# Three one-pass products of 12-bit parts in place of Strassen's float32 products, in a scan followed by a SiLU feed-forward block

## The chip, the cores and the metric

The kernel runs on one core of one Trainium2 chip. The metric is the device time of one execution in microseconds (us). The core's engines are TensorE (PE, with its weight loads listed as PEld), VectorE (DVE), ScalarE (ACT), GpSimd (POOL) and SyncE (SP), whose queue issues most DMAs. Each engine takes its instructions in program order; semaphores tie them together. SBUF is the on-chip memory of 128 partitions, PSUM holds what TensorE writes.

## The reference

A chunked state-space scan, and a two-layer block with SiLU on its output. Cut to what is computed:

```python
x: (4, 8, 768, 32)   a: (4, 8, 768)   B, C: (4, 8, 768, 16)   # batch, heads, tokens, ...
for c in range(768 // 32):                      # per batch and head
    cum = np.cumsum(log(clip(a[c], 1e-6, 1)))
    M = (C[c] @ B[c].T) * np.exp(cum[:, None] - cum[None, :]) * causal
    y[c] = M @ x[c] + (C[c] @ state) * np.exp(cum)[:, None]
    state = exp(cum[-1]) * state + (B[c] * exp(cum[-1] - cum)[:, None]).T @ x[c]
X = y.transpose(0, 2, 1, 3).reshape(3072, 256)
h = X @ w_in                                    # w_in (256, 2048), given in float64
out = (h * sigmoid(h)) @ w_out                  # w_out (2048, 256), given in float64
```

All but the two weight matrices is float32.

## The kernel before, in words

The 3072 tokens are 12 units of 256 tokens (three per batch); two units that follow each other are a pair, so there are six pairs, 0 to 5. For each unit a scan makes the features x tokens matrix XM; then the first product (256 to 2048 features), SiLU, and the second product (2048 to 256).

**Weights.** They arrive as 16 pieces of float64 (`load_w`), and each is turned into float32 by `w_size` (two ScalarE passes) and `w_bits` (three VectorE instructions, L176 to L180, and an add on GpSimd, L184).

**Scan of a unit.** `f_T` or `f_TP` transposes B and C, `f_P` (L285, L291) and `f_E` (L322, L304) make decays by scans on VectorE, `f_B` (L341) and `f_C` (L373) scale B and C, `f_G` and `f_D0` are the products C·B (L406) and the state's increments (L391), `f_M` (L417) multiplies decays in, `f_S` and `f_SM` carry the state, `f_Y` (L460, L469) gives y and `f_X` (L482) copies it out of PSUM. All products of `f_G` of a unit stand in one tile `gy` of four PSUM banks.

**The two products.** Units 0 to 3 have plain first products, `f_s1` (L505, SiLU in L507). Pairs 2 to 5 take their first product by `f_x1` (L703) in Strassen's way: 7 products for 8, with differences of weights (`f_SW`) and of inputs (`f_XT`, L686, GpSimd), copies out of PSUM (L717), sums on VectorE (L706) and SiLU (L709). Every pair's second product is Strassen's too, `s2_pair` (L648; L611 for the first two of pair 0): 7 x 8 products, sums of weights (`f_SO`, L533) and of activations (`f_T1`, L544, and `f_TS`, L553, which adds by DMAs on GpSimd's queue), copies (L588) and sums of results (`p_add`, L558), then a transpose (L564) and four DMAs per output block on SP's queue (`f_out`). All are float32 products over 256 tokens.

**Order.** The order is written out by hand; no scheduler moves anything. The second product of pair P runs between the first products of pair P+1, and the scans of pair P+2's units are spread over the same stretch by `scan_plan`. From pair 2 on, one round of eight j's per pair does all of it.

`busy` (L226, L228) issues bf16 products at the start whose results are not used.

Of the kernel before, what the change touches and what calls it, by code (L numbers as in the profile page):

```python
# [9 lines left out]
U32 = mybir.dt.uint32  # L10
BF16 = mybir.dt.bfloat16
# [6 lines left out]
MOST = 2.0 ** 16 * (1.875 - 2.0 ** -22)  # L18


@with_exitstack
def kernel(
# [22 lines left out]
    nc = tc.nc  # L45
# [13 lines left out]
    loads = ctx.enter_context(tc.tile_pool(name="loads", bufs=3))  # L59
    loads2 = ctx.enter_context(tc.tile_pool(name="loads2", bufs=2))  # L60
    rawp = ctx.enter_context(tc.tile_pool(name="rawp", bufs=7))
    wtp = ctx.enter_context(tc.tile_pool(name="wtp", bufs=3))
    sc = ctx.enter_context(tc.tile_pool(name="sc", bufs=1))
    sc2 = ctx.enter_context(tc.tile_pool(name="sc2", bufs=2))
    xmp = ctx.enter_context(tc.tile_pool(name="xmp", bufs=4))
    gpool = ctx.enter_context(tc.tile_pool(name="gpool", bufs=4))
    tpool = ctx.enter_context(tc.tile_pool(name="tpool", bufs=1))
    ppool = ctx.enter_context(tc.tile_pool(name="ppool", bufs=5))
    opool = ctx.enter_context(tc.tile_pool(name="opool", bufs=2))
    ps_s = ctx.enter_context(tc.tile_pool(name="ps_s", bufs=1, space=bass.MemoryType.PSUM))  # L70
    ps_h = ctx.enter_context(tc.tile_pool(name="ps_h", bufs=3, space=bass.MemoryType.PSUM))
    ps_o = ctx.enter_context(tc.tile_pool(name="ps_o", bufs=1, space=bass.MemoryType.PSUM))

    ctx.enter_context(tc.manual_schedule())


# [5 lines left out]
    def load_pa(u, q):  # L82

        b, t0 = at(u)
        pa[u] = loads.tile([128, UT], FP32, name="pa")
        q.dma_start(out=pa[u], in_=bass.AP(tensor=a.tensor, offset=a.offset + b * H * S + t0,
                                           ap=[[S, H], [0, N], [1, UT]]))

    def load_ab(u, q):

        b, t0 = at(u)
        ab[u] = loads2.tile([128, 2, H, Q], FP32, name="ab")
# [7 lines left out]

# [9 lines left out]

# [7 lines left out]
    def load_x(u, q):  # L118
        b, t0 = at(u)
        xt[u] = loads.tile([128, 2, H, D], FP32, name="xt")  # L120
# [14 lines left out]
    w_in_sb = const.tile([128, KC, d_ff], FP32, name="w_in_sb")  # L135
    w_out_sb = const.tile([128, NF, d_model], FP32, name="w_out_sb")
# [3 lines left out]
    W = [("i", j) for j in range(8)] + [("o", j) for j in range(8)]  # L140
    RAW = 7
    raw, wu, wv = {}, {}, {}

    def w_piece(n):
        which, j = W[n]
        if which == "i":
            return wi[:, :, j * WF:(j + 1) * WF], w_in_sb[:, :, j * WF:(j + 1) * WF]
        return wo[:, 2 * j:2 * j + 2], w_out_sb[:, 2 * j:2 * j + 2]

    def load_w(n, q):  # L150
        src, dst = w_piece(n)
        if src.dtype == FP32:
            q.dma_start(out=dst, in_=src)
            return
        t = raw[n] = rawp.tile([128, 2, WF, 2], U32, name="raw")
        q.dma_start(out=t.rearrange("p k f two -> p k (f two)"), in_=src.bitcast(U32))

    def w_size(n, what="uv"):  # L160
        if n in raw:
            if "u" in what:
                u = wu[n] = wtp.tile([128, 2, WF], FP32, name="wu")
                nc.scalar.activation(u, raw[n][:, :, :, 1].bitcast(FP32), AF.Abs)
            if "v" in what:
                v = wv[n] = wtp.tile([128, 2, WF], FP32, name="wv")

                nc.scalar.activation(v, raw[n][:, :, :, 0], AF.Copy, scale=2.0 ** -51, bias=2.0)

    def w_bits(n, parts=1):  # L170
        dst = w_piece(n)[1]
        if n in raw:
            u, v, hi = wu.pop(n), wv.pop(n).bitcast(U32), raw[n][:, :, :, 1]


# [3 lines left out]

            nc.vector.scalar_tensor_tensor(out=v, in0=hi, scalar=0x80000000, in1=v,  # L180
                                           op0=ALU.bitwise_and, op1=ALU.bitwise_or)
            for i in range(parts):
                fs = slice(WF // parts * i, WF // parts * (i + 1))
                nc.gpsimd.tensor_tensor(out=dst[:, :, fs].bitcast(U32), in0=u[:, :, fs], in1=v[:, :, fs], op=ALU.add)  # L184
        if n + RAW < len(W):
            load_w(n + RAW, nc.sync)


    A0, A1 = 96, 96 + S // Q
    early = gpool.tile([128, NF, UT], FP32, name="gT")  # L190
    ach = early[:, 0:2].rearrange("p a (h t) -> p (a h) t", t=Q)
    nc.sync.dma_start(out=ach[A0:A1], in_=bass.AP(tensor=a.tensor, offset=a.offset, ap=[[Q, S // Q], [S, H], [1, Q]]))

    flat = early.rearrange("p f t -> p (f t)")
    QZ = 8 * (Q + 1)
    pa01 = flat[:, 6 * UT:8 * UT]
    pz01, one01, pfx01 = (flat[:, 8 * UT + QZ * i:8 * UT + QZ * (i + 1)] for i in range(3))
# [16 lines left out]

# [4 lines left out]

    idle = early[:, 4].bitcast(BF16)  # L220
    nc.vector.memset(idle, 0.0)

    def busy(n, small=0):
        t = ps_o.tile([128, 512], FP32, name="o_ps")
# [7 lines left out]
    sel = early[:, 2:4].rearrange("p a (s c t) -> p (a s) c t", s=2, c=2)  # L232
# [4 lines left out]
    diag1 = early[:, 5:6, 0:Q]  # L237
    nc.vector.memset(diag1, 0.0)
    nc.vector.memset(pz01.rearrange("p (c t) -> p c t", c=8)[:, :, 0:1], 0.0)
    nc.vector.memset(one01, 0.0)  # L240
    nc.vector.memset(one01.rearrange("p (c t) -> p c t", c=8)[:, :, 0:1], 1.0)
# [24 lines left out]
    pz = const.tile([128, 4, Q + 1], FP32, name="pz")  # L266
    one = const.tile([128, 4, Q + 1], FP32, name="one")
    for t, n in ((pz, 0.0), (one, 1.0)):
        nc.gpsimd.memset(t, 0.0)
        if n:  # L270
            nc.gpsimd.memset(t[:, :, 0:1], n)
    E, M, BT, BH, CT, CE, CW, PFX, ST, SM, DP, XM, GTS, BX = ({} for _ in range(14))


    def f_P01():

        nc.vector.tensor_scalar(out=pz01.rearrange("p (c t) -> p c t", c=8)[:, :, 1:],
                                in0=pa01.rearrange("p (c t) -> p c t", c=8), scalar1=1.0, scalar2=1e-6,
                                op0=ALU.min, op1=ALU.max)
# [728 lines left out]
```

## Time and profile before

| what | value |
|---|---|
| median of three runs | 351.29 us (350.81 to 354.5) |
| span of the profiled execution | 348.7 us |
| PE / PEld / DVE / ACT / POOL busy | 98 / 83 / 59 / 47 / 32 % of the span |
| granted TensorE clock, mean | 1.000 |
| HBM read, written | 22.70 MB, 3.15 MB |
| DMAs under 512 B, of all packets | 102424 of 117056 |
| first product of pair 0's second layer (L611) | at 50.5 us |
| last matmul group (L626) starts, ends | 342.8, 345.6 us |

The span runs from the first to the last instruction of one execution; it is the only time that the page gives for that execution, and the median of the runs is 2.6 us above it. Busy time of PE counts pipelined matmuls, so two that follow each other overlap in it; the distance between starts tells their rate. Each float32 matmul of the program stands in the trace as two records.

### The profile page before, as it was taken

What the parts mean: (1) busy time and instruction counts of PE and PEld (TensorE: products, weight loads), DVE (VectorE), ACT (ScalarE), POOL (GpSimd) and SP (SyncE); (2) the same over time, 40 slices, a digit from 0 to 9 for tenths busy, and PEclk for the clock granted to TensorE, in tenths of its full rate; (3) what the DMA queues carried; (4) which work ended last, traced back from release to release, by engine and by line L of the source; (5) the groups of instructions that cost most, each with busy time, mean ns of one, the idle gap of its engine ahead of it and who ended that gap; (6) DMA issues with size and microseconds to landing.
All of it is one profiled execution on the core that took longest, in us unless ns stands there. A gap on an engine that the chain in (4) does not pass through costs nothing.

```text
span 348.7 us, 8382 instructions
## 1 busy us (share of the span) xinstructions
PE 342.7 (98%) x3324; PEld 288.5 (83%) x3324; DVE 204.6 (59%) x406; ACT 162.8 (47%) x399; POOL 113.0 (32%) x140
## 2 busy tenths in 40 slices
PE   8999999999999999999999999999999999999996
PEld 3678888888888888888888888888888888888886
DVE  7998799976795664544663563564652241233912
ACT  3578395323323545455645454644545454454010
POOL 4355245444285032244042244042235112041200
DMA  6877997799857598948178965056604237512202
GB/s 130 203 237 174 241 313 126 132 199 218 144 102 126 124 186 149 169 102 138 21 159 163 187 112 90 16 98 125 115 2 75 39 60 144 107 24 53 41 7 46
DMA packets 117056, 42.66 MB, mean 122 GB/s; under 512 B 102424, under 2 KB 108824, under 8 KB 117016
## 3 DMA queue, kind: packets, MB, share of 16 engines
q1 hardware_dynamic: 110472, 25.73, 35.8%
q0 software_dynamic: 4464, 16.25, 25.0%
q8 instruction: 26, 0.43, 0.6%
q10 hardware_dynamic: 2080, 0.13, 0.4%
q14 instruction: 14, 0.11, 0.1%
HBM read 22.70 MB, written 3.15 MB: 74 GB/s over the span
## 4 chain that ended last, share of the span: by engine, by line
PE 96%; DVE 1%; issue 1%; POOL 1%; ACT 0%; DVEq 0%; POOLq 0%
PE o_ps L648 36%; PE hp L703 28%; PE hp L505 16%; PE hp L648 3%; PE gy L469 2%; PE gy L406 2%; PE o_ps L611 2%; PE gy L460 2%; PE gy L391 1%; PE hp L626 1%; PE hp L312 1%; PE o_ps L226 1%; POOL w_in_sb L184 1%; DVE E L417 0%; PE o_ps L228 0%
## 5 line engine op out<-in xcount | busy, mean ns | idle before, releaser
L706 DVE TENSOR_TENSOR gT<-hp,p 128x256 f32<-128x256 f32 x64 | 26.9, 420 | 73.6 <-ACT p L717 37.6
L648 PE MATMUL o_ps<-gT,w_out_sb 128*128 128x256 f32 x240 | 60.4, 379 | 0.0
L709 ACT ACTIVATE gT<-gT 128x256 f32<-128x256 f32 x96 | 39.7, 414 | 43.9 <-DVE gT L706 43.9
L505 PE MATMUL hp<-XM,w_in_sb 128*128 128x256 f32 x256 | 59.3, 381 | 0.9 <-ACT XM L482 0.5
L505 PEld LDWEIGHTS hp<-XM,w_in_sb 128*128 128x128 f32 x256 | 48.0, 190 | 8.7 <-POOL w_in_sb L184 1.4
L703 PE MATMUL hp<-raw 128*128 128x256 f32 x192 | 52.7, 380 | 0.0
L558 POOL TENSOR_TENSOR ps<-ps 128x256 f32<-128x256 f32 x35 | 29.6, 845 | 71.1 <-ACT ps L588 69.8
L648 PEld LDWEIGHTS o_ps<-gT,w_out_sb 128*128 128x128 f32 x240 | 45.4, 190 | 6.3
L553 POOL DMA_DIRECT2D gT<-gT x31 | 27.9, 929 | 65.7 <-DVE TN L544 21.5
L703 PEld LDWEIGHTS hp<-raw 128*128 128x128 f32 x192 | 36.2, 190 | 5.4 <-POOL ps L558 0.6
L717 ACT ACTIVATE p<-hp 128x256 f32<-128x256 f32 x64 | 24.6, 384 | 27.4 <-PE hp L703 25.9
L706 DVE TENSOR_TENSOR gT<-hp,u 128x256 f32<-128x256 f32 x32 | 13.6, 424 | 38.6 <-PE hp L703 38.6
L703 PE MATMUL hp<-XM,w_in_sb 128*128 128x256 f32 x128 | 34.1, 389 | 0.0
L507 ACT ACTIVATE gT<-hp 128x512 f32<-128x512 f32 x32 | 18.9, 595 | 26.4 <-PE hp L505 26.3
L703 PEld LDWEIGHTS hp<-XM,w_in_sb 128*128 128x128 f32 x128 | 23.3, 190 | 4.3 <-issue 1.0
L304 DVE TENSOR_TENSOR_SCAN E<-ab,diag 128x256 f32<-128x256 f32 (+1 forms) x32 | 25.1, 826 | 0.8 <-DVE ab L323 0.5
L341 POOL TENSOR_TENSOR BT<-bn,E 128x256 f32<-128x256 f32 x12 | 9.4, 780 | 47.5 <-DVE E L304 39.4
L648 PE MATMUL o_ps<-gT,wu 128*128 128x256 f32 x88 | 22.4, 380 | 0.0
L648 PE MATMUL o_ps<-gT,wv 128*128 128x256 f32 x88 | 22.2, 380 | 0.0
L648 PE MATMUL o_ps<-gT,raw 128*128 128x256 f32 x80 | 20.5, 380 | 0.0
L588 ACT ACTIVATE ps<-o_ps 128x256 f32<-128x256 f32 x35 | 13.3, 383 | 14.8 <-PE o_ps L648 13.0
L703 PE MATMUL hp<-raw,w_in_sb 128*128 128x256 f32 x64 | 19.1, 380 | 0.0
(126 smaller groups left out, 522.3 us busy)
## 6 DMA issues: line engine op xcount, KB each, us to landing
gT<-gT POOLq DMA_DIRECT2D x31, 512.0 KB, 6.3
ab<-in_a_dram SPq DMA_DIRECT2D x40, 128.0 KB, 3.1
raw<-in_moe_w_in_dram SPq DMA_DIRECT2D x8, 512.0 KB, 5.1
raw<-in_moe_w_out_dram SPq DMA_DIRECT2D x8, 512.0 KB, 6.5
xt<-in_x_dram SPq DMA_DIRECT2D x24, 128.0 KB, 5.1
out_dram<-ot SPq DMA_DIRECT2D x92, 32.0 KB, 2.6
bn<-in_B_dram SPq DMA_DIRECT2D x22, 64.0 KB, 5.3
tbc<-in_C_dram SPq DMA_DIRECT2D x40, 32.0 KB, 3.4
```

Source lines behind the costliest of these rows:

```text
L304: nc.vector.tensor_tensor_scan(out=E[u].rearrange("p k h t -> p (k h t)")[:, Q * g0:Q * (g0 + n)], data0=t.rearrange("p g t -> p (g t)"), ...
L341: engine.tensor_tensor(out=BT[u], in0=bn[u], in1=E[u][:, :, :, Q - 1:Q].to_broadcast([128, 2, H, N]), op=ALU.mult)
L505: nc.tensor.matmul(out=hp[:, i], lhsT=w_in_sb[:, kc, f * 128:(f + 1) * 128], rhs=xm[:, kc], start=(kc == 0), stop=(kc == KC - 1))
L507: nc.scalar.activation(GTS[g][:, :, j], hp, AF.Silu)
L553: nc.gpsimd.dma_start(out=o[:, js], in_=a[:, js], accum_op=ALU.add)
L558: engine.tensor_tensor(out=o, in0=p, in1=q, op=op)
L588: nc.scalar.activation(p[m].rearrange("p (k c t) -> p c k t", c=2, k=2), o.rearrange("p (c k t) -> p c k t", c=2, k=2), AF.Copy)
L648: nc.tensor.matmul(out=o, lhsT=w(j), rhs=g()[:, j], start=(j == 0), stop=(j == last))
L703: nc.tensor.matmul(out=o, lhsT=w, rhs=x_, start=start, stop=True, skip_group_check=True)
L706: nc.vector.tensor_tensor(out=o, in0=p, in1=q, op=ALU.add)
L709: nc.scalar.activation(o, i, AF.Silu)
L717: nc.scalar.activation(o, i, AF.Copy)
```

## The change

Up to the first products of pair 0 the kernel is nearly the same; `f_G` and `f_Y` are cut into halves that use one tile of two PSUM banks in turn. Pair 0 has float32 products still: the first as before, the second plain (8 x 8 products, `f_s2`), after all first products of the pair and not between those of pair 1. From pair 1 on, each float32 matrix is cut into a high part h and a low part l, and a third matrix d is formed: of weights by `w_h` (ScalarE), `w_l` (VectorE), `w_d` (GpSimd); of the scan's output by `f_xh`, `f_xl`, `f_xd` (the same engines, in the order ScalarE, GpSimd, VectorE); of activations by `s1_g` (ScalarE, twice), `s1_gl` (GpSimd), `s1_gd` (VectorE). A product is then made of three products of type float32r over the 512 tokens of a pair. Strassen's form goes, with `f_SW`, `f_XT`, `f_x1`, `f_SO`, `f_T1`, `f_TS`, `p_add` and `s2_pair`. The loads are double buffered instead of triple (xt excepted), and one pool of 66 blocks of 128x512 takes the place of several pools.

The core of the diff (line numbers in the text are those of the new file; L407 is `f_G`'s product, L413 `f_M`):

```diff
-    ps_h = ctx.enter_context(tc.tile_pool(name="ps_h", bufs=3, space=bass.MemoryType.PSUM))
-    ps_o = ctx.enter_context(tc.tile_pool(name="ps_o", bufs=1, space=bass.MemoryType.PSUM))
+    ps_h = ctx.enter_context(tc.tile_pool(name="ps_h", bufs=2, space=bass.MemoryType.PSUM))
+    ps_a = ctx.enter_context(tc.tile_pool(name="ps_a", bufs=4, space=bass.MemoryType.PSUM))
...
+    def w_h(n):
+        WH[n] = block("wh", F32R)
+        nc.scalar.activation(WH[n], w32[n], AF.Copy, scale=DOWN / 4096.0)
+    def w_l(n):
+        WL[n] = block("wl", F32R)
+        nc.vector.scalar_tensor_tensor(out=WL[n], in0=WH[n].bitcast(FP32), scalar=-4096.0, in1=w32.pop(n),
+                                       op0=ALU.mult, op1=ALU.add)
+    def w_d(n, engine=nc.gpsimd):
+        WD[n] = block("wd", F32R)
+        engine.tensor_tensor(out=WD[n], in0=WH[n].bitcast(FP32), in1=WL[n].bitcast(FP32), op=ALU.subtract)
...
+    def f_xh(u):
+        nc.scalar.activation(x_part(XH, u, "xh"), two(XF[u]), AF.Copy, scale=DOWN)
+    def f_xl(u, engine=nc.gpsimd):
+        engine.tensor_tensor(out=x_part(XL, u, "xl"), in0=two(XF.pop(u)), in1=x_part(XH, u, "xh").bitcast(FP32),
+                             op=ALU.subtract)
+    def f_xd(u):
+        nc.vector.scalar_tensor_tensor(out=x_part(XD, u, "xd"), in0=x_part(XL, u, "xl").bitcast(FP32), scalar=-4096.0,
+                                       in1=x_part(XH, u, "xh").bitcast(FP32), op0=ALU.mult, op1=ALU.add)
...
+    def s1_d(s):
+        P, f = 1 + s // NF, s % NF
+        HP[s] = half("hp")
+        for kc in range(KC):
+            nc.tensor.matmul(out=HP[s], lhsT=two(WD[f // 2])[:, kc, 128 * (f % 2):128 * (f % 2) + 128], rhs=XD[P][:, kc],
+                             start=(kc == 0), stop=False, skip_group_check=True)
+        nc.scalar.activation(HP[s], HP[s], AF.Copy, scale=-1.0 / UP)
+    def s1_h(s):
+        for kc in range(KC):
+            for i, (w, x_) in enumerate(((WH, XH), (WL, XL))):
+                nc.tensor.matmul(out=HP[s], lhsT=two(w[f // 2])[:, kc, 128 * (f % 2):128 * (f % 2) + 128],
+                                 rhs=x_[P][:, kc], start=False, stop=(kc == KC - 1 and i == 1), skip_group_check=True)
...
+    def s1_g(s):
+        G[s] = block("g")
+        nc.scalar.activation(G[s], HP.pop(s), AF.Silu, scale=UP)
+        GH[s] = block("gh", F32R)
+        nc.scalar.activation(GH[s], G[s], AF.Copy, scale=DOWN)
+    def s1_gl(s):
+        GL[s] = block("gl", F32R)
+        nc.gpsimd.tensor_tensor(out=GL[s], in0=G.pop(s), in1=GH[s].bitcast(FP32), op=ALU.subtract)
+    def s1_gd(s):
+        GD[s] = block("gd", F32R)
+        nc.vector.scalar_tensor_tensor(out=GD[s], in0=GL[s].bitcast(FP32), scalar=-4096.0, in1=GH[s].bitcast(FP32),
+                                       op0=ALU.mult, op1=ALU.add)
+    def s2(s):
...
+            nc.tensor.matmul(out=OA[P][1][m], lhsT=two(WD[n])[:, r, ms], rhs=gd, start=(f == 0), stop=(f == NF - 1))
...
+            nc.tensor.matmul(out=OA[P][0][m], lhsT=two(WH[n])[:, r, ms], rhs=gh, start=(f == 0), stop=False)
+            nc.tensor.matmul(out=OA[P][0][m], lhsT=two(WL[n])[:, r, ms], rhs=gl, start=False, stop=(f == NF - 1))
+    def f_out(P, m):
...
+            nc.scalar.activation(t, OA[P][1][m], AF.Copy)
+            nc.vector.scalar_tensor_tensor(out=o, in0=OA[P][0][m], scalar=UP, in1=t, op0=ALU.mult, op1=ALU.subtract)
...
+        nc.vector.transpose(out=r, in_=o)
...
+    for text in ("m0 2:h h0 2:l l0 2:d b13 s14", "m1 d0 b14 s15", "m2 h1 b15 3:T", "m3 l1 d1 3:P012", "m4 3:BC 3:G",
+                 "m5 3:Mg 3:m h8 3:D l8 d8", "m6 3:S 3:Y", "m7 3:y 3:h 3:l 3:d h2 l2 d2 h9 l9 d9 o0 o1"):
+        todo(text)
+    LAG = 3
+    PLAN = ("T", "P0", "12GBC", "Mg", "mD", "S", "Y", "y", "hld")
+    def step(s):
...
+            s1_h(s)
+            if s + 1 < last and (s + 1) % NF:
+                s1_d(s + 1)
+            s1_g(s)
+            s1_gl(s)
+        if s >= LAG:
+            s2(s - LAG)
+        if s - 1 >= 0 and s - 1 < last:
+            s1_gd(s - 1)
+        if s >= LAG and (s - LAG) % NF == NF - 1:
+            f_out(P, 0)
+            f_out(P, 1)
...
+        if P + 1 < NP:
+            for i, base in enumerate((0, 6)):
+                if 0 <= f - base < len(PLAN):
+                    u = 2 * P + 2 + i
+                    stage(u, PLAN[f - base])
...
+        if P == 1 and f % 2 == 0:
+            for n in (3 + f // 2, 10 + f // 2):
...
+                    w_h(n)
+                    w_l(n)
+                    w_d(n)
+        if s + 1 < last and (s + 1) % NF == 0:
+            s1_d(s + 1)
```

A letter of PLAN is a part of a unit's scan: T, P, 0, 1, 2 (decays and their two scans), B, C, G and g (the two halves of `f_G`), M and m (of `f_M`), D, S, Y and y (of `f_Y` with its copy), h, l, d (the parts of the scan's output). In the texts above it, b and s are `w_bits` and `w_size`, m0 to m7 the eighths of pair 0's second product, o the outputs. A step s works on 128 hidden features of pair 1 + s // 16; there are 80 steps and three more for the lag.

## The prediction

> **What bounds the kernel now.** I read the busy shares first, then the chain of work that ended last, then a window over one pair of units.
>
> ```profile
> PE 342.7 (98%) x3324; PEld 288.5 (83%) x3324; DVE 204.6 (59%) x406; ACT 162.8 (47%) x399; POOL 113.0 (32%) x140
> ...
> PE 96%; DVE 1%; issue 1%; POOL 1%; ACT 0%; DVEq 0%; POOLq 0%
> ```
>
> TensorE is the bound throughout: 96% of the chain is its own work.
>
> ```profile
> 164.00:218.00 54.00, 54.00 (x530) 45.86 (x529) 28.60 (x67) 27.48 (x74) 15.79 (x21) 1.00 0.66 120
> ```
>
> This is one pair (columns: PE, PEld, DVE, ACT, POOL busy): PE 54.0 of 54.0 us, VectorE 28.6, ScalarE 27.5, GpSimd 15.8. So only fewer PE cycles can help, and the other engines have half of their time to give.
>
> The price of a product, from the timeline of TensorE:
>
> ```profile
> 1.26 2.31 PE L226 MATMUL o_ps<-gT 128*128 128x512 bf16 x5 [1.26 <-DVE gT L221]
> 8.70 0.61 PE L226 MATMUL o_ps<-gT 128*128 128x512 bf16 x2
> 11.02 0.81 PE L226 MATMUL o_ps<-gT 128*128 128x512 bf16 x3
> ...
> 324.39 3.62 PE L648 MATMUL o_ps<-gT,w_out_sb 128*128 128x256 f32 x16
> 327.85 1.89 PE L648 MATMUL hp<-TN,wu 128*128 128x256 f32 x8
> ```
>
> Sixteen float32 records take 327.85-324.39 = 3.46 us, 0.216 each. The program has one instruction for two records, so a float32 product over 256 tokens is 0.432 us and over 512 tokens 0.86. A bf16 product over 512 columns adds 0.81-0.61 = 0.20 (rounding; two pitches of 0.216 fit too).
>
> The other views are those of VectorE and GpSimd side by side:
>
> ```profile
> 48.13 0.43 DVE L178 TENSOR_SCALAR wu<-wu 128x512 uint32<-128x512 uint32 x1
> 56.31 1.39 POOL L184 TENSOR_TENSOR w_out_sb<-wu,wv 128x512 uint32<-128x512 uint32 x1 [0.97 <-DVE wv L180]
> 56.60 1.39 DVE L178 TENSOR_SCALAR wu<-wu 128x512 uint32<-128x512 uint32 x1
> ...
> 101.55 1.34 DVE L675 TENSOR_TENSOR raw<-w_in_sb 128x1024 f32<-128x1024 f32 x1
> 101.77 1.72 POOL L558 TENSOR_TENSOR ps<-ps 128x256 f32<-128x256 f32 x1
> ```
>
> The same VectorE instruction takes 0.43 alone and 1.39 when it starts inside a GpSimd one: it ends 0.29 after GpSimd does. The other way round a GpSimd add of 0.73 takes 1.72 and ends 0.6 after VectorE's. Instructions of the two engines that both go through SBUF twice do not run together. I call that the lock. In the before kernel it costs nothing, because PE does not wait for either.
>
> **The change, part by part.** *PE work.* Pairs 1 to 5 become 80 steps s. A step has 2 products d(s+1) (L520), 4 h(s) (L528), 6 s2(s-3) (L557 to L561), each over 512 tokens. Their type does not occur in the trace: the lower bound is bf16's 0.216, the upper float32's 0.86. I take 0.216, because each is one instruction whose operands hold one part. A step is then 12 x 0.216 = 2.59 us and a pair 41.5, against 2 x 56 x 0.432 = 48.4 now. The scan's small products stay: 12 units x 2.66 (L391 5.4, L406 8.3, L460 7.9, L469 10.3, by 12). Pair 0's second product grows from 56 to 64 float32 products: 27.6 us.
>
> *Vector work removed*: Strassen's sums. 96 L706 (40.5 us), 64 and 32 copies L717 (36.9), 35 L558 (29.6 on POOL), TN 18.0, 31 adding DMAs on POOL's queue (27.9). None was on the chain, so their removal gains nothing by itself.
>
> *Vector work added, per step*: ScalarE three passes of 128x512, scale (L522), silu, gh: 0.60 each by L507 (595 ns), 0.62 from SBUF. GpSimd gl (L542): 1.27 to 1.40 (L184), I take 1.27. VectorE gd (L546), two SBUF inputs: 0.68 (L180, 681 ns). Per weight piece of 11 in pair 1: 0.62 ScalarE, 0.68 VectorE, 1.27 GpSimd. Per unit: xh 0.62, xl 1.27, xd 0.68. Per output block: copy 0.60, add 0.69, transpose between 0.43 (256 wide) and 0.86, taken 0.70. As totals all would fit under 2.59 us a step: 1.8, 1.3 and 0.7. What decides is order: engines take instructions in program order, and the scan's products sit in PE's queue behind waits for VectorE.
>
> *Where PE waits in pairs 2 to 4.* After G(u) in step 2 comes g(u) at the end of step 3, which needs the one gy buffer read by M(u) on VectorE. Ahead of M in VectorE's queue: gd, two output adds and transposes, two scans (L314, 1.2 each), gd. From the start of step 2: gh(2) ends at 3.3, copy 3.95, then 0.7 x 4 = 6.8, scans 9.2, gd 9.9, M 10.6. PE arrives after 2.59+1.3 at its second products, waits 1.4 for the accumulators that the output adds free, ends at 6.6 and waits 4.0 for M. Second unit: in step 8 the queue is xd, scans, gd, M, and xd waits for xl, that for xh, that for gh(8): 3.95 (xh), gl 4.65, xl 5.9, xd 6.65, scans 9.05, gd 9.75, M 10.45. PE arrives at 2.59+0.35+2.59 = 5.5 and waits 4.95. D waits for m twice, 0.5 in all. At the pair's end d(16) needs xd of step 14, ready at 6.65 from that step's start; PE is there at 4.75: 1.9, and then 0.9 for the scale with nothing behind it. Sum of waits 13.8. A pair: 41.5 + 5.3 + 13.8 = 60.6, less 0.14 for each of about 14 hand-overs (0.43-0.29, from the lock rows) = 58.5. Before: 54.0.
>
> *Pair 1.* No output, but 11 weight pieces in steps 0 to 11. Through the lock: gl 12 x 1.27, gd 12 x 0.68, pieces 11 x 1.95, two scans 10.8 (L291 0.70, L285 0.28, L322 0.69, L304 2.4, L341 and L373 1.32), xl and xd 2.0: 57.7 us. Bounds: the w_bits loop at 51 to 58 us ran 2.35 us for rows of 0.41+0.43+0.68+1.27 = 2.79, a factor of 0.84, so 48.6 to 57.7; I take 53, since B and gl also wait in order for the scans. Steps 12 to 15: 10.4, y products 1.5, end wait 2.8, rounded 15. Pair 1: 68.
>
> *Ahead of pair 1.* Until the first second product, now at 50.5: halves of G and Y share one buffer, so PE waits for M (2.1), for SM and X (1.0), and about 1.2 in the first two units: 54.8. Then 27.6 + 2.7 on PE, 3 for g(3) behind w_bits 13 to 15 and five weight pieces (3 x 1.52 + 5 x 0.68 on VectorE, GpSimd 8 x 1.27 between), 0.5 for D, and at the end X, xh, xl, xd, d, scale in a row: 0.5+0.7+1.35+0.75+0.6+0.8 = 4.8. First h at 93.5.
>
> *After.* Pair 5 has no scan: 41.5 + 2.7 for the accumulators = 44.2. Three lagging s2: 3.9. Tail: copy 0.6, two adds and transposes 2.8, 0.2, then 2.8 as now from the last VectorE instruction (345.9) to the end: 6.4.
>
> Sum: 93.5 + 68 + 3 x 58.5 + 44.2 + 3.9 + 6.4 = 391.5 of span, against 348.7. The median of the runs is 351.3, 2.6 above that span, so 394.
>
> *A rule against the change.* The trace has the first five bf16 products at 0.43 us each and later ones at about 0.2, after PE had been idle; PE's later gaps are all under 1.3 us, so the cost of a gap of 4 us or more is unknown: 0 to five slow products, 1.1 us each. I take 0, with 11 such gaps 12 us at most. The Trainium skill, "TensorE: Matmul & The Clock Gate", What's actually happening, says that the array's clock halves after about 3.4 us of idleness and needs as long of work to return. By it each gap would cost up to 1.7 us, some 19 in all (an estimate), and the time would be about 413.
>
> **The rivals.**
> *PE stays the bound and the change wins.* If VectorE and GpSimd run far enough ahead: 52 until pair 0's second product, 27.6 + 2.7 for it and unit 3's scan, 4 for the xh to xd row, 80 x 2.59, 8 scans x 2.66, 5 for the ends of pairs, 10 for lag and tail: 330, 333 with the 2.6 around the span. For it: totals per step are under 2.59, and s2 lags three steps. Against it: g sits only one step after G, and xd is ahead of the scan in the queue. It decides if the scan's chain from gh to M takes under 5.5 us instead of 10.5.
> *In-order waits without the lock for the new instructions* (gd has no bit operation, xl is subtraction): pair 1 near 58, pairs 55.5, first h at 91.5: 91.5+58+166.5+44.2+10.3 = 370.5, 373. Against: L675 is a plain float32 add and shows the lock.
> *The one-pass product takes two passes*, 0.432: 80 x 5.18 = 415, the vector work vanishes beneath, with 93.5 + 21 + 12: 541, 544. Nothing in the trace speaks for it but that the type is unseen.
>
> **How the numbers follow.** Locked, in-order waits (394): 0.74. Waits without lock (373): 0.13. PE bound (333): 0.09. Two passes (544): 0.04. A measurement of this kernel tells about 1% from no change. Faster 0.09, the PE-bound case; same 0.03, out of the no-lock case with small waits; slower 0.88. The range starts at 356, where half of the waits of pairs 1 to 4 ((13.8 x 3 + 25)/2 = 33) and a little more are gone, which holds the no-lock case, and ends at 416, which holds the gap cost of 12 and a pair 1 at 57.7.
>
> **What would show it.** Right: L557/L528 records 0.22 apart; PE busy far under 98%, with gaps of 4 to 5 us before L407 twice a pair, released by VectorE's M (L413); L542 and L546 never overlapping fully, some at twice their length; the first L528 near 93; pair starts 68, then 58 apart. Wrong: gaps before L407 under 1 us, or pairs 47 apart (the PE-bound rival); L528 records 0.43 apart.

## The result, and the profile after

The changed kernel takes 462.5 us (median of four runs, 461.7 to 467.6), the kernel before 351.05 in the same comparison: 1.320 times, interval 1.311 to 1.329. The forecast was 394 with a range to 416. The direction was right; the size was 68 us short. The span of the profiled execution is 460.7 us, against 391.5 in the sum.

From the page of the changed kernel: busy shares, the granted clock in 40 slices, and the chain of work that ended last.

```profile
PE 378.4 (82%) x3145; PEld 284.1 (62%) x3146; DVE 221.4 (48%) x343; ACT 213.1 (46%) x403; POOL 183.5 (40%) x160
...
PEclk9999999977789798879979888979798989889998
...
PE 24%; issue 5%; POOL 4%; ACT 2%; DVE 2%; SPq 1%; DMA 0%; POOLq 0%; ACTq 0%; DVEq 0%
```

PE falls from 98% busy to 82%, and its clock is no longer full: the second line has digits of 7 and 8 in every pair, where the kernel before had a mean of 1.000. Busy PE is itself inflated by this: in the rows below, a product is listed with 0.63 us at a clock of 0.50 and with 0.39 us at full clock.

The same view as was shown of a pair before, now for pair 2 of the changed kernel, with a short window behind its first long wait (columns: us, then PE, PEld, DVE, ACT and POOL busy, PEclk, DMA share, GB/s):

```profile
183.25:256.96 73.71, 62.19 (x504) 46.16 (x504) 29.59 (x50) 33.84 (x64) 26.16 (x22) 0.87 0.24 44
202.00:206.00 4.00, 4.00 (x23) 3.09 (x24) 1.29 (x2) 0.00 (x0) 1.08 (x1) 0.50 0.31 92
```

A pair costs 73.7 us where 58.5 were forecast and 54.0 were needed before. The window at 202 begins where PE comes back from a wait: it is full of work, at a clock of 0.50.

TensorE's timeline of pair 2, the lines around its waits (start, duration, operation, and in brackets the idle time before it and what ended it):

```profile
202.00 1.15 PE L407 MATMUL gy<-ce,bh 32*64 32x128 f32 x16 [4.04 <-DVE E L413]
203.08 0.80 PE L528 MATMUL hp<-xh,wh 128*128 128x512 f32 x1
203.67 0.63 PE L528 MATMUL hp<-xl,wl 128*128 128x512 f32 x1
204.10 0.63 PE L528 MATMUL hp<-xh,wh 128*128 128x512 f32 x1
...
230.39 1.14 PE L407 MATMUL gy<-ce,bh 32*64 32x128 f32 x16 [4.27 <-DVE E L413]
...
255.56 0.73 PE L520 MATMUL hp<-xd,wd 128*128 128x512 f32 x2 [2.54 <-DVE xd L483]
256.96 0.79 PE L528 MATMUL hp<-xh,wh 128*128 128x512 f32 x1 [0.67 <-ACT hp L522]
```

The waits stand where they were forecast, at nearly the forecast sizes (4.0, 4.95, 1.9 and 0.9 were worked out). New is what follows: the products at 203.67 and 204.10 start 0.43 apart. Warm products, from the same view in pair 5:

```profile
412.24 0.39 PE L528 MATMUL hp<-xl,wl 128*128 128x512 f32 x1
412.47 0.39 PE L528 MATMUL hp<-xh,wh 128*128 128x512 f32 x1
```

They start 0.23 apart, not 0.216. Over the whole trace, of 919 distances between two one-pass products that follow each other, 728 are warm (under 0.26 us), with a mean of 0.2317, and 109 are at 0.426; these are called slow from here on. The other 82 stand across a wait, a hand-over or a change of the clock.

The chain on VectorE that ends with M, which the first of these waits is for:

```profile
195.16 0.69 DVE L570 SCALAR_TENSOR_TENSOR o<-oa,od 128x512 f32<-128x512 f32 x1 [1.20 <-ACT od L569]
197.85 2.30 DVE L314 TENSOR_TENSOR_SCAN E<-ab,diag 128x512 f32<-128x512 f32 x2
200.06 0.67 DVE L546 SCALAR_TENSOR_TENSOR gd<-gl,gh 128x512 fp32r<-128x512 f32 x1
201.26 0.69 DVE L413 TENSOR_TENSOR E<-gy,E 128x512 f32<-128x512 f32 x1 [0.53 <-POOL BT L347]
```

Where the 69 us between the sum and the span lie, by the first L528 of each pair:

| stretch | forecast | measured | difference |
|---|---|---|---|
| to the first L528 | 93.5 | 99.4 | 5.9 |
| pair 1 | 68 | 83.9 | 15.9 |
| pairs 2 to 4 | 3 x 58.5 | 217.6 (72.5 each) | 42.1 |
| pair 5, lag, tail | 54.5 | 59.8 | 5.3 |

### The profile page after: what moved, and what is told of

Same layout as the page of the kernel before. It is cut to its first block, busy times and chain, and to the rows that moved or that the text cites. A ratio compares the mean times of both kernels' runs of the same rounds, so it can differ in the third digit from the quotient of the medians.

```text
span 460.7 us, 7904 instructions
## 1 busy us (share of the span) xinstructions
PE 378.4 (82%) x3145; PEld 284.1 (62%) x3146; DVE 221.4 (48%) x343; ACT 213.1 (46%) x403; POOL 183.5 (40%) x160
## 5 line engine op out<-in xcount | busy, mean ns | idle before, releaser
L542 POOL TENSOR_TENSOR gl<-g,gh 128x512 fp32r<-128x512 f32 x80 | 104.2, 1303 | 165.7 <-ACT gh L538 147.4
L546 DVE SCALAR_TENSOR_TENSOR gd<-gl,gh 128x512 fp32r<-128x512 f32 x80 | 61.5, 774 | 142.7 <-POOL gl L542 139.1
L528 PE MATMUL hp<-xh,wh 128*128 128x512 f32 x160 | 75.8, 474 | 12.2 <-ACT hp L522 12.2
L528 PE MATMUL hp<-xl,wl 128*128 128x512 f32 x160 | 70.1, 438 | 0.0
L520 PE MATMUL hp<-xd,wd 128*128 128x512 f32 x160 | 57.7, 446 | 13.5 <-DVE xd L483 13.5
L560 PE MATMUL oa<-gh,wh 128*128 128x512 f32 x160 | 65.8, 411 | 0.4 <-DVE o L570 0.4
L561 PE MATMUL oa<-gl,wl 128*128 128x512 f32 x160 | 65.0, 406 | 0.0
L557 PE MATMUL oa<-gd,wd 128*128 128x512 f32 x160 | 54.6, 424 | 0.1
L407 PE MATMUL gy<-ce,bh 32*64 32x128 f32 x384 | 19.6, 323 | 41.3 <-DVE E L413 41.3
L538 ACT ACTIVATE gh<-g 128x512 fp32r<-128x512 f32 x80 | 50.5, 631 | 3.7
L528 PEld LDWEIGHTS hp<-xh,wh 128*128 128x128 f32 x160 | 33.9, 212 | 28.0 <-ACT hp L522 16.5
L520 PEld LDWEIGHTS hp<-xd,wd 128*128 128x128 f32 x160 | 34.0, 215 | 23.6 <-DVE xd L483 15.4
L536 ACT ACTIVATE g<-hp 128x512 f32<-128x512 f32 x80 | 47.5, 593 | 1.0 <-PE hp L528 0.6
L407 PEld LDWEIGHTS gy<-ce,bh 32*64 32x64 f32 x384 | 12.7, 155 | 49.9 <-DVE E L413 42.8
L528 PEld LDWEIGHTS hp<-xl,wl 128*128 128x128 f32 x160 | 34.4, 215 | 5.9
```

The lines of the kernel that those rows point to most:

```text
L407: nc.tensor.matmul(out=GY[u][64 * c:64 * c + 64, q, 128 * k:128 * k + 128], lhsT=bh[32 * g:32 * g + 32, ts], rhs=ce[32 * g:32 * g + 32, :, ...
L520: nc.tensor.matmul(out=HP[s], lhsT=two(WD[f // 2])[:, kc, 128 * (f % 2):128 * (f % 2) + 128], rhs=XD[P][:, kc], start=(kc == 0), stop=Fals ...
L528: nc.tensor.matmul(out=HP[s], lhsT=two(w[f // 2])[:, kc, 128 * (f % 2):128 * (f % 2) + 128], rhs=x_[P][:, kc], start=False, stop=(kc == KC ...
L536: nc.scalar.activation(G[s], HP.pop(s), AF.Silu, scale=UP)
L538: nc.scalar.activation(GH[s], G[s], AF.Copy, scale=DOWN)
L542: nc.gpsimd.tensor_tensor(out=GL[s], in0=G.pop(s), in1=GH[s].bitcast(FP32), op=ALU.subtract)
```

## The experiments

All times below are medians of the runs of one comparison; each kernel is the changed kernel with the edit shown. The ratios are to the kernel before, which was run again in each comparison (medians 350.8 to 351.05); the changed kernel was not, and differences to it are taken to its 462.5.

**Is it standing still that makes the next products slow?** Theory: TensorE loses its clock over each wait, and that loss is the term taken as 0. Rival: the products after a wait are slow for another reason, or the waits are simply longer. The first try put products of zeros into the waits:

```
+        if u > 3 and i == 1:
+            fill(LAST[u], 34)      # into the unused columns of the gy tile
...
+            fill(bank2(), 22)      # before a pair's first s1_d
```

> The changed kernel with bf16 products of zeros, whose results are not used, put on TensorE where it idles: 34 of 256 columns (3.6 us) ahead of each second half of f_G in pairs 1 to 4, 22 (2.4 us) ahead of each pair's first d product. Theory 'clock': the gaps make TensorE slow after them; in the changed kernel's pair 2 the products after its three gaps start 0.43 us apart instead of 0.232, in all some 10 us. With the gaps filled they start 0.232 apart, pairs 2 to 4 shrink from 73 us to 63 to 65, pair 1 by 5 to 8, the whole from 462.5 to 420 to 430. Rival 'data': the products after a gap are slow for another reason, such as operands just written; then they stay at 0.43 and the time is 462 or a little more.

486.5 us (484.0 to 488.7), 24 slower than the changed kernel. TensorE's timeline shows why:

```profile
209.17 6.39 PE L242 MATMUL gy<-zt 128*128 128x256 bf16 x34 [4.04 <-DVE E L425]
```

The filling products share the gy tile that M (here L425) reads, so they waited for M themselves: the wait of 4.04 is still there, and 6.39 us of filling stand behind it, the first 3.3 of them at a clock of 0.50. The time of this run says nothing on the theory, since no wait got shorter. Its distances do: now the zeros are what runs slowly, and of the one-pass products behind them not one in pairs 2 to 4 is slow (20 are left, all in pair 1). What was slow in this run is what came first after a wait, whatever its operands. The second version writes the hp bank that the step after next overwrites, which nothing late holds:

```
+        for i in range(n):
+            nc.tensor.matmul(out=HP[s][:, 0:UT], lhsT=zt[:, 0:128], rhs=zt, start=True, stop=True)
...
+                    if PLAN[f - base] == "Mg":
+                        fill(s + 2, 34)
...
+            fill(s + 1, 22)
             s1_d(s + 1)
```

> 34 bf16 products of zeros with 256 columns stand before the second half of each unit's products of bh and ce in pairs 1 to 4, and 22 before each pair's first product of xd. They write the hp bank that the next step's product writes over, so they wait for nothing that comes late. If the slow products behind a gap come from TensorE having stood still, the gaps stay as long (41.3 us in all before L407, 13.5 before L520) but what follows them runs at 0.233 us a product: 8 x 3.3 and about 4 x 2 us less, 425 to 435. If they are slow for another reason (GpSimd's or VectorE's traffic at that moment), the time stays within 4 us of 462.5.

439.7 us (439.5 to 439.9): 22.8 less, ratio 1.251 (1.246 to 1.256). The expected 425 to 435 was too good by 5. The 30 slow products that are left all stand in pair 1: 20 behind waits that were not filled (for loads, and the first one for xd), 10 behind one of which 3.7 us stayed unfilled. The same place as in the changed kernel, in the timeline of this one (it begins behind the first of the 34 products of zeros):

```profile
195.80 3.77 PE L244 MATMUL hp<-zt 128*128 128x256 bf16 x33
199.89 0.68 PE L416 MATMUL gy<-ce,bh 32*64 32x128 f32 x16 [0.32 <-DVE E L422]
200.84 0.39 PE L538 MATMUL hp<-xl,wl 128*128 128x512 f32 x1
201.07 0.40 PE L538 MATMUL hp<-xh,wh 128*128 128x512 f32 x1
```

The products of zeros deliver nothing, and M keeps L407 waiting as long as before (195.80 to 199.89, where the changed kernel stood still for 4.04), and yet the products behind run 0.23 apart and the 16 products of L407 take 0.68 instead of 1.15. Over the trace the slow products fall from 109 to 30, 79 x 0.195 = 15.4 us; the scan's small products and the first products behind a wait gain as well. Work whose results are thrown away made the kernel faster by 23 us; the theory stands.

**Which place in the order makes the waits?** The first unit's xd is in front of the second unit's decay scans on VectorE; it was moved two steps later:

```
-    PLAN = ("T", "P0", "12GBC", "Mg", "mD", "S", "Y", "y", "hld")
+    PLAN = ("T", "P0", "12GBC", "Mg", "mD", "S", "Y", "y")
+                if f == (10, 14)[i]:
+                    stage(2 * P + 2 + i, "hld")
```

> The changed kernel with the first unit's parts h, l, d formed in step 10 instead of step 8 of a pair, so that xd no longer stands ahead of the second unit's scans in VectorE's queue. Theory 'order in the queue': the second wait for M in each pair (4.3 us in the changed kernel) falls to under 1 us, and with it the slow products after it (about 3 us): 7 us in each of pairs 2 to 4, at least as much in pair 1: 462.5 becomes 430 to 437. Rival 'the lock or the amount of vector work sets the pair': the wait moves to another place and the time stays within 5 us of 462.5.

468.1 us (466.5 to 468.4): 6 slower by the medians, with a ratio of 1.327 to 1.338 against 1.311 to 1.329, so that no more is sure than that it is not faster. The waits of TensorE after 95 us, in sum (columns: waiting line, releaser, us in total, times, longest), the changed kernel first:

```profile
PE gy L407 <- DVE E L413: 38.7, 8, 7.9
```

and with xd moved:

```profile
PE gy L407 <- DVE E L413: 22.5, 6, 6.2
PE gy L392 <- issue: 16.8, 4, 4.4
```

16 us of L407's waits went and 16.8 came back before L392: xd now stands on VectorE ahead of the second M, which D (L392) needs, and waits 4.35 us there for GpSimd's xl. That is the rival that a moved instruction moves its wait. The scans were then moved themselves, one step ahead of the products they serve:

```
-    PLAN = ("T", "P0", "12GBC", "Mg", "mD", "S", "Y", "y", "hld")
+    PLAN = ("T", "P012B", "GCM", "gm", "D", "S", "Y", "y", "hld")
```

> Each later unit's two decay scans are recorded one step earlier, ahead of its first products of bh and ce, and the multiplication by them in the step before the second products. If the waits before those second products are the scans' place on VectorE, and each also costs some 3.3 us of slow products, the 41.3 us before L407 fall to about 6 and 8 x 3.3 us go with them: 400 to 408. If the gaps cost no more than themselves, 425 to 430. If the wait only turns up before another product, as it did when the first unit's xd was moved, 455 to 468.

433.8 us (433.1 to 435.9), 28.7 less. L407 waits 15.1 us in all instead of 38.7 and no other wait grew by more than 1.8, so the wait did not move. These 23.6 us of waits and 27 slow products fewer (82 remain, 27 x 0.195 = 5.3) come to 28.9. The time lies near the second expectation, which took a wait to cost no more than itself, but by chance: fewer of the waits went than it supposed, and at that price the time would have been 438.9. What is left stands behind xd: in the trace the second unit's scans are now ahead of the first unit's xd, and M is directly behind it (one wait of 6.9 in pair 1, where xd runs from 154.49 and M from 155.57).

**Does GpSimd hold VectorE up?** The prediction priced pair 1 and the steps by the lock between the two engines.

```
-        nc.gpsimd.tensor_tensor(out=GL[s], in0=G.pop(s), in1=GH[s].bitcast(FP32), op=ALU.subtract)
+        nc.vector.tensor_tensor(out=GL[s], in0=G.pop(s), in1=GH[s].bitcast(FP32), op=ALU.subtract)
```

> The subtraction that makes gl goes from GpSimd to VectorE, 80 times. GpSimd loses 104 us of work, VectorE gains 80 x 0.67 = 54 us (the duration of its like, gd). If the two engines hold each other up (gd's row at 774 ns where the shortest were 670, xd 1106, L302 1090), gd falls to 670 to 690 ns, L302 to about 700, and the time falls by 5 to 15 us, to 447 to 457. If the order on VectorE is what decides, the scans and the multiplications by the decays stand behind 54 us more of work, the waits before the second products of each unit grow by 0.7 to 1.4 us each, and the time rises to 465 to 475.

500.9 us (495.9 to 502.0), 38 slower, and outside both expectations. gd did not shorten (827 ns, before 774). VectorE's timeline of pair 2:

```profile
222.28 0.69 DVE L542 TENSOR_TENSOR gl<-g,gh 128x512 fp32r<-128x512 f32 x1 [5.88 <-ACT gh L538]
222.88 0.68 DVE L546 SCALAR_TENSOR_TENSOR gd<-gl,gh 128x512 fp32r<-128x512 f32 x1
223.49 0.68 DVE L413 TENSOR_TENSOR E<-gy,E 128x512 f32<-128x512 f32 x1
```

gl waits for gh of its own step, which ScalarE can make only when TensorE has finished that step's h; M (L413), whose input was there long before, stands behind it. On GpSimd the same wait is in front of nothing that the scan needs at once. So this place on VectorE costs 38 us, and a lighter GpSimd did not make up for it. By itself the run does not test whether instructions of the two engines lengthen each other, since VectorE got the work that GpSimd lost; the rows of the changed kernel say more on that (below).

**The wait in pair 1 that was not in the prediction.** From the timelines of SP's queue, VectorE and TensorE:

```profile
99.28 4.40 SPq L574 DMA_DIRECT2D out_dram<-ot  x8
108.07 0.64 DVE L352 STREAM_TRANSPOSE bh<-tbc 128x256 f32<-128x256 f32 x1 [8.22 <-DMA tbc<-in_B_dram]
112.82 0.80 PE L528 MATMUL hp<-xh,wh 128*128 128x512 f32 x1 [8.18 <-ACT hp L522]
```

Pair 0's outputs go to the queue first, and unit 4's loads behind them; the transposes of B and C stand on VectorE until these land, with wl and gd behind them, and TensorE stands 8.2 us. The loads were put ahead of the outputs:

```
-    ... d2 h9 l9 d9 o0 o1"):
+    ... d2 h9 l9 d9 4:L o0 o1 5:L"):
-    stage(4, "L")
-    stage(5, "L")
```

> The changed kernel with the loads of unit 4 issued ahead of pair 0's outputs on SyncE's queue, not behind them. Theory 'queue': the 8.2 us for which VectorE waits for unit 4's B in pair 1's first steps go, and TensorE's wait of 8.2 us with them: 462.5 becomes 451 to 456. Rival 'the vector work of pair 1 decides': pair 1 stays near 84 us, since the weight pieces fill the time, and the whole is within 3 us of 462.5.

457.15 us (454.9 to 460.5), 5.4 less, ratio 1.303 (1.2961 to 1.3107; the interval of the changed kernel begins at 1.3109, so the two only just miss each other). The wait of 8.2 is gone (the longest left before L528 is 0.7) and that is the clearer sign of the two. That not all of it came back fits the slow products of pair 1, 34 where there were 20.

**All waits together.** Scans as above, the loads ahead, and h, l, d one step earlier (`"Y", "yhld"` at the end of PLAN):

> The scans earlier as in the run before, the loads of unit 4 ahead of pair 0's output transfers, and the parts h, l and d of each unit one step earlier. If all three waits are separate, this takes 6 to 8 us for the loads and 2.6 us and some slow products at the end of each pair off 400 to 408: 380 to 392. If the wait at a pair's end is the chain from the last y to xd and does not shrink, 392 to 400. If the scans' wait only moves, 440 to 455.

412.95 us (412.8 to 414.4), ratio 1.176 (1.171 to 1.181): 49.6 less, and 21 more than the expected 380 to 392. That expectation was built on 400 to 408 for the scans alone, which had been missed by 26. Of the 49.6, the scans alone gave 28.7 and the loads 5.4; 15.5 are left for the parts at the pairs' ends, if the three add up. TensorE's longest sums of waits after 95 us:

```profile
PE gy L407 <- DVE E L413: 16.4, 8, 5.7
PE hp L528 <- ACT hp L522: 4.7, 7, 0.7
```

Pair 2 now runs at a granted clock of 1.00 in 59.6 us:

```profile
171.89:231.50 59.61, 54.36 (x504) 40.48 (x504) 30.85 (x50) 34.08 (x64) 27.29 (x23) 1.00 0.29 54
```

Two attempts at what was left. Products of zeros before the second unit's L407, with another bank for the transposes of the opening:

```
+                    if PLAN[f - base] == "gm" and i == 1:
+                        fill(s + 2, 24)
-        tp = half("tp")
+        tp = acc("tp")
```

> Scans, loads and parts as in the combined run (412.95), and also 24 bf16 products of zeros with 256 columns before the second unit's second products of bh and ce, where 5.7 us of waiting are left in pair 1 and about 2.7 in the others, and the transposes of units 1 to 3 through a bank of their own instead of one of the two hp banks. If the slow products after these four waits still cost 1.6 to 3 us each, 7 to 10 us go, and 2 us of the opening with the bank: 401 to 405. If waits of 2.7 us cost nothing behind themselves, 409 to 412.

411.9 us (410.6 to 414.1), not told from 412.95. Slow products: 42 against 43. In pairs 2 and 3 of the run without filling there was nothing to regain, as its timeline shows, where the products behind a wait of 2.70 are warm:

```profile
210.31 0.68 PE L407 MATMUL gy<-ce,bh 32*64 32x128 f32 x16 [2.70 <-DVE E L413]
210.92 0.50 PE L528 MATMUL hp<-xh,wh 128*128 128x512 f32 x1
211.26 0.39 PE L528 MATMUL hp<-xl,wl 128*128 128x512 f32 x1
```

and in pair 1 the 24 products cover 2.6 of 5.7 us, too little. The other attempt, without products of zeros but with that bank, has two buffers for the decays and puts the second unit's scans ahead of the first unit's y and xd:

```
-            E[u] = sc.tile([128, 2, H, Q], FP32, name="E")
+            E[u] = sc2.tile([128, 2, H, Q], FP32, name="E")
-            for i, base in enumerate((0, 6)):
+            for i, base in ((1, 6), (0, 0)):
```

> Without the products of zeros: scans, loads, parts and bank as in the combined runs, two buffers for the decays E (64 blocks instead of 66 to make room), and the second unit's scans recorded ahead of the first unit's last y and xd. If the scans standing behind xd are what is left of the waits, the four waits of 2.7 to 5.7 us fall under 1 us each and their slow products go: 395 to 400. If the multiplication by the decays is now behind xd instead, 406 to 412.

409.1 us (407.9 to 411.1): pair 3 fell from 61.1 to 58.6, pair 2 rose from 59.6 to 60.4, and the opening of the profiled execution was 2.7 shorter. L407 still waits 15.2 us in all (7.0 in pair 1), so the scans behind xd were not what is left. VectorE's timeline of pair 2 shows what is:

```profile
203.50 1.77 DVE L483 SCALAR_TENSOR_TENSOR xd<-xl,xh 128x512 fp32r<-128x512 f32 x1 [2.09 <-POOL xl L479]
205.19 1.16 DVE L546 SCALAR_TENSOR_TENSOR gd<-gl,gh 128x512 fp32r<-128x512 f32 x1
206.28 0.68 DVE L413 TENSOR_TENSOR E<-gy,E 128x512 f32<-128x512 f32 x1
```

M now stands behind xd, as the second expectation (406 to 412) had it; xd waits for GpSimd's xl, and beside GpSimd's work it takes 1.77 and gd 1.16 where 0.69 and 0.67 were seen above. This version has the lowest median of all (its interval meets that of the run before it), and it is 1.165 times the time before (1.159 to 1.171).

**The opening.** Only the bank of the transposes:

```
-        tp = half("tp")
+        tp = acc("tp")
```

> Only the bank of the transposes in the opening is changed (one of the four accumulator banks in place of one of the two hp banks). If TensorE's wait of 1.84 us for cw there is the sharing of the bank, the first oa product comes 2 us earlier (59.4 instead of 61.4) and the time falls to 460 to 461; if the order on VectorE and ScalarE sets it, another wait takes its place and the time stays at 462 to 463.

462.5 us (460.3 to 465.3), no change. The wait of 1.84 us for cw is gone, and from the waits before L445 at 28.92 and 60.38 in the changed kernel to the same two in this one (33.76 and 63.06) the stretch fell from 31.5 to 29.3; but this execution came to the first of them 4.8 us later. The first L528 of the profiled kernels whose openings are the same lies between 99.4 and 103.2. The 6 us of the opening can't be told apart within that.

**The pitch of a product.** Rows of products were appended behind the last step of the changed kernel, with warm rows of 40 behind waits of growing length:

```
+    row(40, wb, wb[:, 512:1024])              # bf16
+    row(24, WH[0], WL[0])                     # float32r
...
+    o = row(40, WH[0], WL[0])
+    for n in range(1, 9):
+        c = link(o, n)                        # a chain of n copies on ScalarE
+        o = row(40, WH[0], c)
```

> The changed kernel with rows of products behind its end, whose results are not used, to measure their distance: float32r with changing and with one repeated set of weights, float32r of 256 columns, bf16 of 256 and 512 columns; then eight rows of 40 float32r products, each behind an idle time made by one to eight ScalarE copies in a chain (about 0.7 us each). Theory 'a fixed cost of the type': float32r takes 0.232 with any weights, 0.125 for 256 columns, and bf16 0.216 and 0.107. Theory 'weights': with repeated weights float32r falls to 0.216. Of the gaps, theory 'a fixed threshold of about 3.4 us' (the Trainium skill, TensorE: Matmul & The Clock Gate, What's actually happening) expects full speed after gaps of up to 3 us, and 0.43 for about 3.4 us after longer ones. The changed kernel's gap of 2.6 us, after which products stood 0.43 apart for 6 us, speaks against that; the rival is that any gap over about 2 us slows some 3 to 7 us of products.

Only the rows are read (the whole took 610 us). The waits, in TensorE's timeline:

```profile
456.08 8.79 PE L762 MATMUL row<-wb 128*128 128x512 bf16 x39 [3.11 <-DVE wb L755]
506.98 9.37 PE L762 MATMUL row<-link,wh 128*128 128x512 f32 x40 [1.35 <-ACT link L770]
518.36 10.99 PE L762 MATMUL row<-link,wh 128*128 128x512 f32 x40 [2.01 <-ACT link L770]
561.45 12.04 PE L762 MATMUL row<-link,wh 128*128 128x512 f32 x40 [3.99 <-ACT link L770]
```

Forty products take 9.37 us after a wait of 1.35 (9.36 after 0.69), 10.99 after 2.0 to 3.4, and 12.04 after 4.0: 1.6 and 2.7 us lost, by 7 to 8 and by 12 products at 0.427. That is the price of a wait in rows of float32r products. It isn't set by the wait's length alone: behind the 2.01 the first four products are still warm and the slow ones come after them, and behind the wait of 3.11 ahead of a bf16 row, in the same execution, none is slow (granted clock 1.00; the first two records, with one of the row's 40 missing from the trace, stand 0.43 apart, all others 0.216). Float32r rows settle at 0.227 a product, with four weight blocks in turn as with one, and bf16 at 0.216.

For the 0.0157 us between 0.2317 and 0.216, the products of the steps were given the upper halves of the same words as bf16 (`t.bitcast(BF16)` with every second element, weights and columns; the products are then those of parts with their lower halves cut off):

> The changed kernel with its 960 one-pass products reading the upper halves of the same float32 words as bf16 (every second 16-bit word), so the products are those of the rounded-off parts; everything else is as it was. If the type costs 0.2325 a product against bf16's 0.216, 960 x 0.0165 = 15.8 us less, 446 to 449. If the pitch comes from the operand's 4-byte stride or from the other engines' traffic, the time stays within 4 of 462.5.

455.3 us (453.9 to 457.7): 7.2 less, between the two, with a warm pitch of 0.2268. So the last run measured type, stride and traffic each by itself, in appended rows:

> The changed kernel with rows of products appended behind its last step; only these rows are read, not the time. With the other engines still: bf16 products with 128x128 weights and 512 columns, both operands packed, or the weights, the columns or both read as every second 16-bit word; then float32r; then three rows of 70 float32r products beside which ScalarE, VectorE and GpSimd in turn work through a chain of 14 blocks of 128x512 that lasts about half of the row. If the type sets the pitch, all four bf16 rows run at 0.216 and float32r at 0.227. If the 4-byte stride does, the strided bf16 rows run at 0.227 too. If traffic adds the rest up to the 0.2317 of the kernel's steps, the first half of one of the last three rows is slower than its second by 0.005.

From TensorE's timeline of it:

```profile
452.40 13.76 PE L763 MATMUL row<-wl,wh 128*128 128x512 f32 x60
466.00 8.81 PE L763 MATMUL row<-wb 128*128 128x512 bf16 x39
474.64 8.80 PE L763 MATMUL row<-wb,wh 128*128 128x512 bf16 x39
483.28 9.20 PE L763 MATMUL row<-wl,wb 128*128 128x512 bf16 x39
492.31 71.31 PE L763 MATMUL row<-wl,wh 128*128 128x512 bf16 x313
```

The last line runs together the bf16 row with both operands strided and all float32r rows after it. Distances of starts: 60 float32r products take 466.00 - 452.40 = 13.60, 0.2267 each; 40 packed bf16 ones 8.64, 0.216; with strided weights 8.64, the same; with strided columns 9.03, 0.2258. The columns' 4-byte stride, then, makes 0.0098 of the 0.0157 and the type about 0.001. The chains of ScalarE, VectorE and GpSimd beside the last three rows changed nothing: 0.2267 in both halves of each (GpSimd's chain lasted as long as its row). The 0.005 left between 0.2267 and the steps' 0.2317 (960 x 0.005 = 4.8 us) went when the steps read bf16 words at the same stride (0.2268), so in the steps the type costs more than in a row; why stays open.

## Why the prediction was right and wrong

**Right: the mechanism and the waits.** TensorE is no longer the bound because M comes late by VectorE's order. The waits in pair 2 were 4.04 and 4.27 before L407 (forecast 4.0 and 4.95), 2.54 for xd (1.9) and 0.67 for the scale (0.9). The worked chain from the first output add to the end of M was 6.65 us; VectorE's rows give 195.16 to 201.95, 6.79. Moving the scans (28.7 us) confirmed the cause. The closeness is in part luck. The chain holds a wait of 0.53 that the sum had not: M writes over E, and GpSimd's BT, which reads E, takes 1.00 beside gd. The waits for accumulators (1.4) and for D (0.5) hardly showed. The listed waits add up to 13.65, not 13.8.

**The lock, in the rows of pairs 2 to 4.** In both chains to M VectorE's instructions take what they take alone (gd 0.67, a scan 1.15, M 0.69), so there the order does it. At the pair's end the lock shows: beside GpSimd's gl, xd takes 1.73 us (253.77 to 255.50) where the first unit's took 0.69, about 1.0 of that wait of 2.54.

**Wrong, first step: "I take 0" for what a wait costs behind itself, "12 us at most".** It costs 1.6 to 2.7 us behind the float32r rows' waits from 2.0 us on, and 23 us in the kernel were regained by filling the waits. Counted in the trace: 109 products x (0.426 - 0.2317) = 21.2, and the scan's small products behind a wait are slow too. The bound was set from five slow products seen at the kernel's start; a wait of 4 us makes twelve. The prediction also quoted the Trainium skill, "TensorE: Matmul & The Clock Gate", What's actually happening, against itself: the clock halves after about 3.4 us of idleness, up to 1.7 us a wait, 413 in all by its estimate. The rule was right in kind and a better guess than 0, but the runs differ from its figure on both sides: a loss is seen from 2.0 us of waiting on, and is 2.7 at 4.0. The page also says that the window of activity runs freely; in the run with all waits shortened, three waits of 2.7 were followed by 0, 0 and 6 slow products, which agrees with that. In pair 3 of that run five slow products even stand behind three short waits close together (0.94, 0.34 and 0.59), which in pairs 2 and 4 cost nothing.

**Wrong, second step: "I take 0.216".** Each product took 0.2317: 960 x 0.0157 = 15.1 us. Taking the lower bound of an unseen form left no room above it.

**Wrong, third step: the scan's products at 5.3 us a pair.** They were summed from the busy times of their groups. In the run with all waits shortened, pair 2 is 59.6 us; less 192 products x 0.2317 = 44.5, less the bracketed waits of 5.2, 9.9 us remain for the scan's products and the changes to and from them. That is 4.6 a pair more, 18 in all four.

**Not shown: the credit of 0.14 a hand-over**, 2 us a pair, taken from the lock's rows. No run shows it. The waits less this credit are 11.8 in the forecast and 11.5 in the trace, so it did no harm to the sum; that the missing waits of 1.9 and the credit of 2 cancel is luck.

With the three steps, pair 2 adds up: 44.5 + 9.9 + 11.5 of waits + 29 slow products x 0.195 = 5.7 makes 71.6; the 2.1 left fit the scan's own products at half the clock (L407 alone 2 x 0.47) and the first products behind each wait. The measured pair is 73.7.

**Pair 1** was costed as GpSimd and VectorE holding each other, 53 + 15. The 83.9 measured are TensorE's 54.4 of work and 25.9 of waits (8.2 behind the loads, 5.9 and 7.9 before L407, 2.6 and twice 0.67 at the ends), and 20 slow products. The missing item was a queue: unit 4's loads stand behind pair 0's outputs on SP. The two waits before L407 are longer there than the 4.0 and 4.3 of pair 2, where no weight pieces are made; whether by the lock or by order was not tried. The lock is in its rows: L330, 0.67 us in pair 2, takes 1.72 at 147.36, and gd 1.79 at 142.65.

**The rivals.** No case on record held 462. "TensorE stays the bound and the change wins" is not only not what happened, by these figures it could not have: warm and with no wait at all, a pair is 44.5 + 9.9 = 54.4 us, against 54.0 before, and the opening is 11 us longer up to the first second-layer product (61.4 against 50.5). Its 333 rested on the same 0.216 and 2.66 a unit. The two-pass rival fell with the first L528 rows 0.23 apart.

## What to carry to other kernels

Price a wait of TensorE as its own length plus what follows: for waits of 2 us and more, 1.6 to 2.7 us each is what was seen here as a rule (23 us for the twelve that were filled), with exceptions both ways, and count them per loop round; filling a wait that can't be removed with work that waits for nothing late returns that part. When an engine's instruction is moved, look at what then stands behind it in the same queue and what it waits for itself (moving gl or xd moved a wait or made a longer one; moving the loads, which have nothing to wait for, removed one). And before counting waits, sum the bound engine's own work by distances of starts, hand-overs included: here that sum alone, 54.4 against 54.0 a pair, says that the change had nothing to win.

## What was not expected of the hardware

- A product's pitch depends on the stride of the moving columns, not of the weights: 0.216 us packed bf16, 0.2258 with columns at a 4-byte stride, 0.2267 float32r, all for 128x128 weights and 512 columns.
- In rows of float32r products the clock's loss begins between 1.35 and 2.0 us of waiting, and comes in two sizes: 1.6 us up to 3.4 us of waiting, 2.7 from 4.0 on. Length alone does not decide: a wait of 3.11 ahead of a bf16 row was free, in the kernel a wait of 2.7 was free twice of three times, and three waits of under 1 us within 3 us were once followed by five slow products.
- Chains of ScalarE, VectorE or GpSimd work beside float32r products left the pitch at 0.2267.
